# Attention values of 18 late pairs of tiles computed from rounded halves by three products instead of one full-precision product

## The chip, the cores and the metric

The kernel runs as one program on one core of a Trainium2 chip. The metric is device time in microseconds (us) of one execution, the median of several runs. A profiled execution has, beside its own time, a span: from the first to the last instruction that the trace shows. The engines are TensorE (PE, with its weight loads as PEld), VectorE (DVE), ScalarE (ACT), GpSimd (POOL) and SyncE (SP, which here only starts DMA transfers). Each works through its own list of instructions in order; semaphores make one wait for another.

## The reference

Attention over channels, then a mixture of experts with a greedy assignment by the sorted gate values:

```python
qn = q / (norm(q, axis=1) + 1e-6)            # q, k, v: (4, 5056, 256), float32
kn = k / (norm(k, axis=1) + 1e-6)
a = softmax(kn.transpose(0, 2, 1) @ qn / tau)   # 256 x 256 per batch
x = (v @ a).reshape(20224, 256)              # the attention values
logits = x @ w_gate                          # 8 experts
for idx in argsort(-logits.flatten()):       # greedy, at most 2528 tokens per expert
    tok, e = idx // 8, idx % 8
    if assigned[tok] < 0 and counts[e] < cap: assigned[tok] = e; counts[e] += 1
for e in range(8):
    out[assigned == e] = relu(x[assigned == e] @ w1[e]) @ w2[e]
```

The assignment depends on tiny differences of the gate values, so they are computed in full precision. The values x and the expert layers only have to be close to float32.

## The kernel before, in words

**Scores and gates.** For each of the four batches the kernel streams q and k, forms the 256 x 256 score matrix, the softmax and a matrix a that also holds the 8 gate columns (`a_f[b]`). Batch and chunk number name a piece of the tokens: (b, c) with 5 chunks of 1024 tokens per batch (8 tiles of 128). `L` collects the gate values of all tokens.

**Values.** v @ a is done per pair of tiles (`x_tiles`, lines 207 to 221): two tiles, each with two matmuls of 128 x 128 weights (v) and 256 moving columns (a) in float32, into one PSUM tile `px` (four of these rotate). The trace shows each float32 matmul as two PE instructions. ACT copies the pair to the chunk tile `xs` (two rotate), and after four pairs a DMA started by ACT stores the chunk into `x_d` in DRAM (`store_x`). The last 13 chunks, 52 pairs, are the list `TODO`; they run on PE while the routing of the first expert runs on DVE.

**Routing.** `route(p, R)` picks the tokens of one expert by two 16-ary searches for a threshold, four steps each. A step is: DVE compares all keys with 15 thresholds (`ge`, line 556), PE counts by 20 small matmuls (line 525), DVE reduces (`Dm`, `Dr`, `Ex`), PE sums by one matmul (line 538), DVE finds the new threshold (`mxs`, `hit`, `thr`, `cur`, `pre`). A ninth count follows. Then `ei`, the number of the expert, is known (its weights are loaded, `load_w`, on POOL's queue), and `compact` makes the list of its tokens: PE products `pi` (line 734), counted by ACT and DVE, then `src` (list to gather by) and `idx` (list to scatter by). Then the route of the next expert starts, beside the current expert's layers.

**Experts.** Each expert has 20 columns of 128 tokens, in chunks (the first expert: 2, 4, 4, 4, 4, 2 columns; the others five times 4). A column is gathered from `x_d` by an indirect DMA of POOL (`xg`, line 1032; 128 rows of 1 KB). A chunk is turned to channel-major by PE transposes (`turn`, line 1176, into the one PSUM tile `pt`) or by DVE and two DMAs, and split into a high half (ACT, rounded to fp32r) and a low half (DVE, the rest). A layer is three fp32r products, high by high, high by low, low by high: `layer1` (line 1219, 512 moving columns) and `layer2` (line 1253, 24 matmuls of 128 x 256 per column). ACT copies a column's result to `y`, and POOL scatters it with an indirect DMA (line 1262). Expert weights are split in the same way (`split_piece`: 4 pieces of 512 columns for each of w1 and w2; ACT line 1008, DVE line 1011).

**What sets the order.** All instructions are written out by one Python program that keeps a model of PE's and DVE's clocks (`Order`). `tick` moves the model's PE clock, and `hook` slips in whatever a stream (the route, the compaction) has ready by the model: DVE work by priority, PE work when its input is due. So each engine's list is fixed at build time, and where the model is wrong the chip waits. POOL's list is part of it: after each scatter of layer 2 one gather is taken from a queue (`gather`), and in layer 1 one for every second block of 128 hidden channels; with a list done, `load_ahead` puts the next chunk's columns into that queue. `next_turn` puts the transposes of the next expert's first chunk into the last chunk of layer 2 once the list is done and 7.5 us of the model's time have passed (`GATHER_LAT`).

## Time and profile before

| | |
|---|---|
| median of 3 runs | 1283.24 us (1282.59 to 1284.38) |
| the profiled execution's own time | 1284.13 us |
| its span | 1282.4 us |
| granted TensorE clock, mean | 0.996 |
| start to the last 13 chunks (scores, first chunks) | 0 to 231.7 us |
| last 13 chunks and the start of the first expert | 231.7 to 345.2 us |
| expert layers | 345.2 us to the end |

A row of the timeline gives start (us), length (us), engine, line, operation, output<-inputs, shapes and count, and in brackets how long the engine had been idle and what it waited for. A row of the windows gives a stretch, its length, and the busy time (and the number of instructions) of PE, PEld, DVE, ACT and POOL, then the granted clock, the DMA share and GB/s. A row of the waits reads: who waited for whom, us in total, times, longest.

### The profile page before, as it was taken

The numbers are of one execution on the slowest core, as the hardware profiler recorded it, in microseconds if no ns is written. First come the engines' busy times: TensorE is split into PE (matmuls) and PEld (weight loads), VectorE is DVE, ScalarE is ACT, GpSimd is POOL, SyncE is SP. The second block draws the span as 40 slices with busy tenths as digits, with TensorE's granted clock in tenths as the row PEclk, the third lists the DMA queues.
The fourth block names the chain that finished last, engine by engine and source line by source line (L and its number), as shares of the span: only waits on it lengthen the run. The fifth ranks groups of instructions, "written<-read, shape, count | busy, mean of one in ns | idle before, by whom it ended". The sixth has DMA issues, their size and how long they took to land.

```text
span 1282.4 us, 23001 instructions
## 1 busy us (share of the span) xinstructions
PE 1263.7 (99%) x8878; PEld 1124.4 (88%) x8878; DVE 806.3 (63%) x1992; ACT 530.0 (41%) x1197; POOL 388.9 (30%) x616
## 2 busy tenths in 40 slices
PE   7999999999999999999999999999999999999998
PEld 6888877787789998898999898988998998899998
DVE  6766396758677766967776787687665434344421
ACT  5554452225233443534443444354345434343331
POOL 1000010000152363265227333623543443433122
PEclk9999999999999999999999999999999999999999
DMA  8999885235324123333313341442352334323110
GB/s 297 359 402 351 298 280 194 73 129 197 124 86 144 38 78 107 116 102 111 132 60 118 101 161 39 151 159 67 104 167 78 114 101 148 109 71 109 64 52 33
DMA packets 80414, 180.38 MB, mean 141 GB/s; under 512 B 10800, under 2 KB 50608, under 8 KB 75696
## 3 DMA queue, kind: packets, MB, share of 16 engines
q1 hardware_dynamic: 41248, 99.63, 22.5%
q0 software_dynamic: 17664, 58.22, 13.9%
q10 hardware_dynamic: 21392, 21.06, 4.8%
q8 instruction: 69, 1.13, 0.4%
q14 instruction: 41, 0.34, 0.1%
HBM read 118.58 MB, written 60.29 MB: 139 GB/s over the span
## 4 chain that ended last, share of the span: by engine, by line
PE 85%; issue 8%; POOL 3%; DMA 3%; ACT 1%; DVE 1%; SPq 0%; POOLq 0%; ACTq 0%
PE ph L1219 30%; PE py L1253 29%; PE s L266 10%; PE px L216 10%; PE pc L525 3%; POOL out_dram L1262 2%; DMA ua<-in_q_dram 1%; PE px L371 1%; DMA x_d<-xs 1%; PE pi L734 0%; POOL xg L1032 0%; PE pt L734 0%; PE pm L356 0%; PE pc L284 0%; PE pc L538 0%
## 5 line engine op out<-in xcount | busy, mean ns | idle before, releaser
L1253 PE MATMUL py<-ua,hH 128*128 128x256 f32 (+1 forms) x2560 | 453.4, 280 | 0.0
L1219 PE MATMUL ph<-xH,ua 128*128 128x512 f32 (+3 forms) x1312 | 407.2, 386 | 0.1
L1253 PEld LDWEIGHTS py<-ua,hH 128*128 128x128 f32 (+1 forms) x2560 | 389.7, 187 | 2.3
L1253 PE MATMUL py<-ua,hL 128*128 128x256 f32 (+1 forms) x1280 | 356.5, 279 | 0.0
L1227 DVE SCALAR_TENSOR_TENSOR hL<-ph,hH 128x512 fp32r<-128x512 f32 (+3 forms) x328 | 219.3, 669 | 190.0 <-ACT hH L1222 186.6
L1262 POOL DMA_INDIRECT out_dram<-y,idx x160 | 161.7, 1011 | 445.4 <-ACT y L1260 388.8
L1222 ACT ACTIVATE hH<-ph 128x512 fp32r<-128x512 f32 (+3 forms) x328 | 190.9, 582 | 226.5 <-PE ph L1219 218.7
L1219 PEld LDWEIGHTS ph<-xH,ua 128*128 128x128 f32 x1312 | 242.9, 188 | 45.2 <-ACT xH L1178 0.6
L1219 PE MATMUL ph<-xL,ua 128*128 128x512 f32 (+3 forms) x656 | 253.1, 386 | 0.3 <-DVE xL L1181 0.2
L1253 PEld LDWEIGHTS py<-ua,hL 128*128 128x128 f32 (+1 forms) x1280 | 239.0, 187 | 0.0
L1260 ACT ACTIVATE y<-py 128x256 f32<-128x256 f32 (+1 forms) x160 | 61.4, 384 | 317.9 <-PE py L1253 274.3
L1032 POOL DMA_INDIRECT xg<-x_d,src x160 | 164.9, 1030 | 88.3 <-DVE Ex L534 42.9
L266 PE MATMUL s<-ua 128*128 128x256 f32 (+1 forms) x640 | 147.3, 390 | 7.4 <-DMA ua<-in_q_dram 7.2
L266 PEld LDWEIGHTS s<-ua 128*128 128x128 f32 (+1 forms) x640 | 123.6, 195 | 29.1 <-issue 12.0
L1219 PEld LDWEIGHTS ph<-xL,ua 128*128 128x128 f32 x656 | 123.3, 188 | 22.2 <-DVE xL L1181 0.8
L216 PE MATMUL px<-a,vr 128*128 128x256 f32 (+1 forms) x448 | 104.8, 389 | 0.1
L275 ACT ACTIVATE sq<-ua 128x1024 f32<-128x1024 f32 (+1 forms) x80 | 76.4, 969 | 58.8 <-DMA ua<-in_k_dram 22.4
L216 PEld LDWEIGHTS px<-a,vr 128*128 128x128 f32 x448 | 84.1, 193 | 12.0
L220 ACT ACTIVATE xs<-px 128x512 f32<-128x512 f32 (+1 forms) x96 | 50.0, 527 | 93.5 <-PE px L216 90.6
L1109 DVE TENSOR_TENSOR xL<-xT,xH 128x512 fp32r<-128x512 f32 (+1 forms) x72 | 47.5, 678 | 30.5 <-ACT xH L1106 30.3
L276 DVE TENSOR_TENSOR acc_k<-acc_k,sq 128x1024 f32<-128x1024 f32 (+2 forms) x40 | 44.4, 1114 | 27.1 <-ACT sq L275 25.9
L293 POOL TENSOR_SCALAR ny<-ny 128x4 f32<-128x4 f32 x4 | 1.3, 324 | 193.2 <-ACT ny L292 193.2
(284 smaller groups left out, 1136.8 us busy)
## 6 DMA issues: line engine op xcount, KB each, us to landing
x_d<-xs ACTq DMA_DIRECT2D x19, 1024.0 KB, 5.0
ua<-in_k_dram SPq DMA_DIRECT2D x35, 512.0 KB, 7.2
ua<-in_q_dram SPq DMA_DIRECT2D x35, 512.0 KB, 9.0
via<-xs SPq DMA_DIRECT2D x35, 512.0 KB, 2.9
xT<-via SPq DMA_DIRECT2D x140, 128.0 KB, 3.2
vr<-in_vt_dram SPq DMA_DIRECT2D x14, 1024.0 KB, 10.4
ua<-in_vt_dram SPq DMA_DIRECT2D x4, 1024.0 KB, 4.7
xg<-x_d,src POOLq DMA_INDIRECT x160
```

The lines of the kernel that those rows point to most:

```text
L216: mm = PE.matmul(px[:, i * C:i * C + width], lhsT=vs[b, c][:, kb, t + i, :], rhs=a_f[b][:, kb, 0:width], start=(kb == 0), stop=(kb == 1))
L220: S.activation(xs[:, t:t + n, 0:width], px[:, 0:n * width].rearrange("p (t c) -> p t c", t=n), AF.Copy)
L266: newest[0] = PE.matmul(sb[:, ib * C:(ib + 1) * C], lhsT=kt[:np_, t, ib * 128:(ib + 1) * 128], rhs=qt[:np_, t, :], start=(first and t == 0 ...
L275: S.activation(sq[:n, t0:t1], t_[:n, t0:t1], AF.Square)
L1032: P.indirect_dma_start(out=xg[:n, i, :], out_offset=None, in_=x_d, in_offset=bass.IndirectOffsetOnAxis(ap=idx[:n, col:col + 1], axis=0))
L1109: V.tensor_tensor(xL[:, kb, 0:k * 128].rearrange("p (i t e) -> p i t e", i=k, t=4), rows, xH[:, kb, 0:k * 128].rearrange("p (i t e) -> p i ...
L1219: PE.matmul(ph[:, 0:nt], lhsT=l[:, w], rhs=x_[:, kb, 0:nt], start=(i == 0), stop=(i == 5))
L1222: S.activation(hH[:, fb, 0:nt], ph[:, 0:nt], AF.Relu)
L1227: V.scalar_tensor_tensor(hL[:, fb, 0:nt], ph[:, 0:nt], 0.0, hH[:, fb, 0:nt].bitcast(F32), op0=OP.max, op1=OP.subtract)
L1253: PE.matmul(py[:n, 0:C], lhsT=l[:, fb, tk], rhs=w[:, d], start=(j == 0), stop=(j == 23))
L1260: S.activation(y[:n], py[:n, 0:C], AF.Copy)
L1262: sd = P.indirect_dma_start(out=out, out_offset=bass.IndirectOffsetOnAxis(ap=idx[:n, col:col + 1], axis=0), in_=y[:n], in_offset=None)
```

## The change

For chunks of batches 1 and 2 in `TODO`, once nine pairs have passed, a pair can be computed from halves (`x_halves`): v and a are each rounded to fp32r by ACT (`hi`, line 254 of the new kernel), the rest is formed by DVE (`lo`, line 256), and a pair is 12 fp32r matmuls (line 269) instead of 4 float32 ones. A stream (`halver`) makes the halves: its DVE step is of a new kind "L", which competes with the other streams as if it started 350 ns later (`YIELD`), at the lowest priority. Four pairs' halves fit in a ring on two of the tiles named `ua`; the halves of a (`a_hi`, `a_lo`) are in a new pool. A pair whose halves are not written by the time PE reaches it is computed as before. It comes to 18 such pairs; the list holds 20 high and 20 low halves of v and two of each for a, so two pairs of halves are made and not used. `TODO` starts with (3, 3) and (3, 4) now, whose tiles the ring takes over, and of the first expert's weights only the four pieces of w1 are split within the values; the four of w2 follow after the last pair.

```diff
@@ constants
-TODO = ((3, 1), (3, 2), (3, 3), (3, 4), (1, 2), (1, 3), (1, 4), (2, 0), (2, 1), (2, 2), (2, 3), (2, 4), (3, 0))
+TODO = ((3, 3), (3, 4), (3, 1), (3, 2), (1, 2), (1, 3), (1, 4), (2, 0), (2, 1), (2, 2), (2, 3), (2, 4), (3, 0))
+HALVED = (1, 2)
+RING = 4
+YIELD = 350
@@ after x_tiles
+    parts_a = {}
+    hv = []
+    ring = []
+    halved = {}
+    gone = []
+    live = []
+
+    def halver(work):
+        n = 0
+        for w in work:
+            while w not in gone and (len(gone) < 9 or len(live) >= RING):
+                yield "W", 0
+            if w in gone:
+                continue
+            b, c, t = w
+            if not ring:
+                for i in (2, 3):
+                    ring.append(ffw.tile([128, 2048], F32, name=f"ua{i}").bitcast(F32R)
+                                .rearrange("p (s h a t n) -> p s h a t n", s=2, h=2, a=2, t=2))
+            todo = []
+            if b not in parts_a:
+                parts_a[b] = [hv[0].tile([128, 2, C], F32R, name=x, bufs=2) for x in ("a_hi", "a_lo")]
+                todo.append((a_f[b][:, :, 0:C], parts_a[b]))
+            slot = ring[n // 2 % 2][:, n % 2]
+            n += 1
+            live.append(w)
+            todo.append((vs[b, c][:, :, t:t + 2, :], (slot[:, 0], slot[:, 1])))
+            for x, (hi, lo) in todo:
+                S.activation(hi, x, AF.Copy)
+                yield "L", 700
+                V.tensor_tensor(lo, x, hi.bitcast(F32), op=OP.subtract)
+            if w in gone:
+                live.remove(w)
+            halved[w] = todo[-1][1]
+
+    def x_halves(b, c, t, xs, tick):
+        px = ps_x.tile([128, 512], F32, name="px")
+        aH, aL = parts_a[b]
+        vH, vL = halved[b, c, t]
+        for i in range(2):
+            j = 0
+            for kb in range(2):
+                for l, r in ((vH, aH), (vH, aL), (vL, aH)):
+                    PE.matmul(px[:, i * C:(i + 1) * C], lhsT=l[:, kb, i, :], rhs=r[:, kb, :], start=(j == 0), stop=(j == 5))
+                    j += 1
+                    tick(C / 2.4 + 10)
+        S.activation(xs[:, t:t + 2, 0:C], px.rearrange("p (t c) -> p t c", t=2), AF.Copy)
@@ Order.hook
-                        c = (max(self.dve, st.mine) if eng == "V" else self.dve, st.prio(), st)
+                        c = ((max(self.dve, st.mine) if eng == "V" else self.dve) + (YIELD if eng == "L" else 0), st.prio(), st)
...
-                        self.dve = best[0] + st.next[1]
+                        self.dve = best[0] + st.next[1] - (YIELD if st.next[0] == "L" else 0)
@@ the last 13 chunks
+        hv.append(actx.enter_context(tc.tile_pool(name="hv", bufs=1, side="right")))
+        o.add(halver([(b, c, t) for b, c in TODO if b in HALVED for t in range(0, T, 2)]), lambda: 9)
         for i, (b, c) in enumerate(TODO):
             xs = vp.tile([128, T, GW], F32, name="xs", bufs=2)
             for t in range(0, T, 2):
-                x_tiles(b, c, t, xs, C, o.tick)
+                gone.append((b, c, t))
+                if (b, c, t) in halved:
+                    x_halves(b, c, t, xs, o.tick)
+                    live.remove((b, c, t))
+                else:
+                    x_tiles(b, c, t, xs, C, o.tick)
                 settle()
-                if cut_w[0] and o.pe > cut_w[0][0] and len(cut_w[0]) > 1:
+                if cut_w[0] and o.pe > cut_w[0][0] and len(cut_w[0]) > 1 and cut_w[0][1][0] == 0:
                     split_piece(0, *cut_w[0].pop(1))
```

Since all lists are written anew, other places move too. Three of them matter below.

VectorE, one step of the first search. Before:

```order
L556 TENSOR_TENSOR ge_1567<-hi_1598,thr_1686 128x10x120 x2
L567 TENSOR_SCALAR pre_1697<-steps_136,cur_1688 128x15
L528 TENSOR_TENSOR Dm_1725<-pc_1703,dmask_132 128x64
L531 TENSOR_REDUCE Dr_1728<-Dm_1725 128x8
L534 TENSOR_TENSOR Ex_1630<-Dr_1728,jsel_129 120x128
L545 TENSOR_REDUCE mxs_1736<-pc_1703 128x15
```

Now (ua2 and ua3 are the ring with the halves of v, vr a chunk of v):

```order
L607 TENSOR_TENSOR ge_1567<-hi_1601,thr_1696 128x10x120 x2
L618 TENSOR_SCALAR pre_1707<-steps_136,cur_1698 128x15
L256 TENSOR_TENSOR ua2_1677<-vr_726,ua2_1677 128x512 x2
L579 TENSOR_TENSOR Dm_1739<-pc_1713,dmask_132 128x64
L582 TENSOR_REDUCE Dr_1742<-Dm_1739 128x8
L585 TENSOR_TENSOR Ex_1633<-Dr_1742,jsel_129 120x128
L256 TENSOR_TENSOR ua3_1678<-vr_726,ua3_1678 128x512
L596 TENSOR_REDUCE mxs_1750<-pc_1713 128x15
```

Low halves stand in the two gaps of a step, ahead of `Dm`, which waits for the count on PE, and ahead of `mxs`, which waits for the sum.

GpSimd, from the last columns of the first expert's layer 2 on, where the second expert's list is done (scatters of `y` at line 1262, then 1313; gathers of `xg` at 1032, then 1083). Before, from the 13th scatter on (`xg_4071` is the second expert's first chunk, `xg_4072` its second; the copies to `spacer` tie a gather to a block of layer 1):

```order
L1262 DMA out_0_dram<-y_4067,idx_2504 20224x256
L1032 DMA xg_4071<-x_d_66,src_4000 128x256
L1261 MEMSET spacer_1566 1x1
L1262 DMA out_0_dram<-y_4113,idx_2504 20224x256
L1032 DMA xg_4071<-x_d_66,src_4000 128x256
L1043 COPY spacer_1566<-hH_4118 1x1
L1032 DMA xg_4071<-x_d_66,src_4000 128x256
L1043 COPY spacer_1566<-hH_4118 1x1
L1032 DMA xg_4071<-x_d_66,src_4000 128x256
L1043 COPY spacer_1566<-hH_4118 1x1
L1032 DMA xg_4072<-x_d_66,src_4000 128x256
```

Now, from the 17th scatter on (`xg_4400` is the second expert's first chunk, `xg_4401` its second; its first two gathers stand behind the 15th and 16th scatter):

```order
L1313 DMA out_0_dram<-y_4483,idx_2686 20224x256
L1083 DMA xg_4400<-x_d_66,src_4373 128x256
L1312 MEMSET spacer_1566 1x1
L1313 DMA out_0_dram<-y_4538,idx_2686 20224x256
L1083 DMA xg_4400<-x_d_66,src_4373 128x256
L1312 MEMSET spacer_1566 1x1
L1313 DMA out_0_dram<-y_4585,idx_2686 20224x256
L1083 DMA xg_4401<-x_d_66,src_4373 128x256
L1312 MEMSET spacer_1566 1x1
L1313 DMA out_0_dram<-y_4649,idx_2686 20224x256
L1083 DMA xg_4401<-x_d_66,src_4373 128x256 x3
L1083 DMA xg_4402<-x_d_66,src_4373 128x256 x4
```

The list comes two scatters later, and from there one gather goes with each scatter: the first chunk's fourth gather stands behind the 18th scatter, the second chunk's last three behind the 20th.

TensorE, around the 19th and 20th column of the first expert's layer 2 (`py_4543` and `py_4598`), where the first half of the second expert's first chunk is turned (`pt_4592`). Now:

```order
L1304 MATMUL py_4543<-ua2_2818,hH_4244 128x256
L1304 MATMUL py_4543<-ua3_2819,hH_4244 128x256
L1304 MATMUL py_4543<-ua2_2818,hL_4245 128x256
L1227 MATMUL pt_4592<-identr_72,xg_4400 128x128 x4
L1304 MATMUL py_4598<-ua2_2818,hH_4244 96x256
L1304 MATMUL py_4598<-ua3_2819,hH_4244 96x256
```

The four transposes, one for each gathered column, stand ahead of the 20th column as before; the second half is turned behind it, and the first half of the second chunk (`xg_4401`) after two blocks of layer 1, both as before. Further on, the third expert's second chunk is turned by eight PE transposes now (two times four, in layer 1), where DVE and DMAs turned it before; the list of PE has 44 transposes of `xg` instead of 36.

## The prediction

> **What bounds the kernel now.** I read the page first: busy time, and the chain of work that ended last.

> ```profile
> PE 1263.7 (99%) x8878; PEld 1124.4 (88%) x8878; DVE 806.3 (63%) x1992; ACT 530.0 (41%) x1197; POOL 388.9 (30%) x616
> PE 85%; issue 8%; POOL 3%; DMA 3%; ACT 1%; DVE 1%; SPq 0%; POOLq 0%; ACTq 0%
> ```

> TensorE is busy 99% of the span and carries the chain. So time goes down only where PE's list gets shorter, and every wait of PE that is added goes into the total. Then the windows, for the stretch of the first search and for the expert layers (length, then PE, PEld, DVE, ACT, POOL busy), and the longest of PE's waits between 231.7 and 345.2 us:

> ```profile
> 245.60:292.00 46.40, 46.40 (x374) 40.85 (x372) 28.38 (x108) 13.73 (x23) 0.00 (x0) 1.00 0.40 136
> 345.20:1282.40 937.20, 930.60 (x7052) 847.70 (x7051) 573.03 (x1456) 379.51 (x954) 370.64 (x580) 1.00 0.31 100
> ```

> ```profile
> PE pi L734 <- ACT ext L755: 2.1, 1, 2.1
> ```

> In the search PE is never idle, while DVE has 18.0 us free and ACT 32.7. Behind it PE is idle 6.6 us in 937, so nothing there absorbs a new wait.

> **The pairs.** First the copies of two pairs that no search step interrupts (ACT), then three matmuls of layer 2, whose shape (fp32r, 128 x 128 weights, 256 moving columns) is that of the new products:

> ```profile
> 233.74 0.60 ACT L220 ACTIVATE xs<-px 128x512 f32<-128x512 f32 x1 [6.89 <-PE px L216]
> 235.46 0.60 ACT L220 ACTIVATE xs<-px 128x512 f32<-128x512 f32 x1 [1.13 <-PE px L216]
> ```

> ```profile
> 386.23 0.39 PE L1253 MATMUL py<-ua,hH 128*128 128x256 f32 x2
> 386.45 0.28 PE L1253 MATMUL py<-ua,hL 128*128 128x256 f32 x1
> 386.57 0.39 PE L1253 MATMUL py<-ua,hH 128*128 128x256 f32 x2
> ```

> A pair takes 1.72 us now. Three products take 386.57 - 386.23 = 0.34, twelve 1.36. The gain is 0.36 a pair, **6.5 us** for 18.

> **The halves in the search.** A step of DVE, with PE's rows for the same step, and a high and a low half of the same size (weights, 128 x 512):

> ```profile
> 248.74 1.48 DVE L556 TENSOR_TENSOR ge<-hi,thr 128x1200 bf16<-128x1200 int16 x2
> 250.13 0.23 DVE L567 TENSOR_SCALAR pre<-steps,cur 128x15 f32<-128x15 f32 x1
> 251.55 0.23 DVE L528 TENSOR_TENSOR Dm<-pc,dmask 128x64 f32<-128x64 f32 x1 [1.19 <-PE pc L525]
> ...
> 252.99 0.28 DVE L545 TENSOR_REDUCE mxs<-pc 128x15 f32<-128x120 f32 x1 [0.58 <-PE pc L538]
> ```

> ```profile
> 250.76 0.75 PE L525 MATMUL pc<-oh,ge 128*128 128x64 bf16 x20
> ...
> 255.86 0.75 PE L525 MATMUL pc<-oh,ge 128*128 128x64 bf16 x20
> ```

> ```profile
> 318.30 0.62 ACT L1008 ACTIVATE ua<-ub 128x512 fp32r<-128x512 f32 x1
> 318.95 0.69 DVE L1011 TENSOR_TENSOR ua<-ub,ua 128x512 fp32r<-128x512 f32 x1
> ```

> A step is 5.1 us, and DVE idles 1.19 + 0.58 = 1.77 of it. Within the nine counts stand 20 low halves, 13.8 us by the row against 15.9 of gaps. Two ahead of `Dm` need 1.38 where 1.19 is free, one ahead of `mxs` 0.69 where 0.58 is: 0.3 over in a full step. The cover is that PE starts the count at 250.76, 0.54 behind the end of `ge` (250.22). What can break it is a low half that waits for its high half: ACT's list holds that behind a copy of a pair. A whole copy late (0.60) makes such a step 0.3 + 0.6 - 0.54 = 0.36 longer, eight steps 2.9; with no low half late the price is 0. PE's list has the counts at about the old spacing (10 float32 matmuls, or 37 to 38 products). Behind a waiting count stand the next pairs, so the wait is paid in full. I take **0.8**, nearer to the covered case, since DVE's total fits, and 0.2 for the second expert's first count, which stands five matmuls (5 x 0.43 = 2.2 us) nearer to the list's products than before, while three low weight halves (2.1) left DVE ahead of it. Together **1.0**, between 0 and 3. ACT's 22 high halves, 22 x 0.62 = 13.6, fit into its free time.

> **Stores and the end of the values.** Page, part 6, and the rows from the last store to the first chunk's transposes (ACT's queue, POOL, PE):

> ```profile
> x_d<-xs ACTq DMA_DIRECT2D x19, 1024.0 KB, 5.0
> ```

> ```profile
> 336.38 0.37 ACTq L226 DMA_DIRECT2D x_d<-xs  x1
> ```

> ```profile
> 339.73 0.95 POOL L1032 DMA_INDIRECT xg<-x_d,src  x1 [42.92 <-DVE Ex L534]
> 340.99 0.95 POOL L1032 DMA_INDIRECT xg<-x_d,src  x1 [0.30 <-issue]
> ```

> ```profile
> 343.79 0.28 PE L1176 MATMUL pt<-identr,xg 128*128 128x128 f32 x1 [0.76 <-DMA xg<-x_d,src]
> ```

> A chunk of four halved pairs takes 5.4 us without any step's PE work, and the copy that needs its `xs` tile back comes a pair later, at 6.8; a store lands in 5.0, so nothing waits. The 2.1 us wait for `ext` hangs on a store beside the weights' loads, which keep their place behind the search; I leave it. From the last store to the transposes the chain is store, gather, landing, all unchanged, so a gain of PE ahead of it comes through. The four pieces of w2 are split in that time now: one high half and four low ones, 0.62 + 4 x 0.69 = 3.4 us from 336.75, end at 340.1 on engines that are next needed after 343.79. They cost nothing; without that cover it would be 2.8. They issue no transfer. The new list for gathering stays far ahead:

> ```profile
> 323.33 0.18 DVE L832 COPY_PREDICATED src<-early,w__2476 128x20 int32<-128x20 int32 x1
> ```

> It is done 16.4 us before the first gather, and the gain takes at most 6.5 of that.

> **The second expert's gathers.** This is the place where I expect the gain to go. The lists show that its first chunk's fourth gather stands behind the 18th scatter now, and its second chunk's last three behind the 20th. The trace of before has both slots with other gathers in them. ACT's copy of the 18th column and POOL:

> ```profile
> 463.10 0.38 ACT L1260 ACTIVATE y<-py 128x256 f32<-128x256 f32 x1 [3.15 <-PE py L1253]
> ```

> ```profile
> 463.76 0.97 POOL L1262 DMA_INDIRECT out_dram<-y,idx  x1 [0.74 <-ACT y L1260]
> 465.04 0.97 POOL L1032 DMA_INDIRECT xg<-x_d,src  x1 [0.30 <-issue]
> ...
> 470.32 0.93 POOL L1262 DMA_INDIRECT out_dram<-y,idx  x1 [1.40 <-ACT y L1260]
> 471.56 0.98 POOL L1032 DMA_INDIRECT xg<-x_d,src  x1 [0.30 <-issue]
> ```

> And PE's transposes of the two chunks:

> ```profile
> 465.68 0.46 PE L1176 MATMUL pt<-identr,xg 128*128 128x128 f32 x4
> 465.97 0.45 PE L1253 MATMUL py<-ua,hH 128*96 128x256 f32 x2
> ...
> 469.47 0.50 PE L1176 MATMUL pt<-identr,xg 128*128 128x128 f32 x4
> ...
> 473.33 0.46 PE L1176 MATMUL pt<-identr,xg 128*128 128x128 f32 x4
> ```

> A gather that starts at 340.99 releases PE at 343.79: 2.80 us. The gather at 465.04 would release its transpose at 467.84, and PE is there at 465.68 + 0.2 for the other three: **1.9 us** of waiting. The next ones start at 471.56, and 1.26 apart (339.73, 340.99), the third at 474.08; it releases PE at 476.88, and PE is there at 473.33 + 0.2: **3.3 us**. The first wait moves the second place's scatter as well, so both are paid. Were the data there as POOL's 0.95 ends, the waits would be 0.1 and 1.5; a scatter can take 0.6 longer, then 2.5 and 3.9. I take 5.2, from the one row that has a landing, between 1.6 and 6.4.

> [...]

> **More transposes.** Eight more, two groups of 465.97 - 465.68 = 0.29: **0.6**.

> **Sum.** -6.5 + 1.0 + 5.2 + 0.6 = **+0.3 us**. The profiled execution took 1284.13 us, 1.73 more than its span and 0.89 more than the median; the change adds to either, so on the median 1283.24 it gives **1283.5**.

> **Rivals.**
> (a) The gathers are hidden anyway: the full gain stays, less the search and the transposes. For it: the model lets 7.5 us pass between the list and the turning. Against it: what is late is the queue of one gather per scatter, not the list. -6.5 + 1.0 + 0.6 = -4.9: 1278.3; with the waits at their low end, 1279.9.
> (b) Slower: the search becomes the bound. In each step the low halves at both gaps wait a whole copy: 0.3 + 1.2 - 0.54 = 0.96, eight steps 7.7 in place of 0.8, so +7.2: 1290.4. It decides from 0.39 a step on (3.1 in eight, then the total is over +2.6). For it: high halves are put on ACT just ahead of their low halves. Against it: ACT is busy 30% of that stretch, and a copy waits only for its pair.
> (c) The products do not run at 0.113. The page's weight loads of this shape last 0.187:

> ```profile
> L1253 PEld LDWEIGHTS py<-ua,hH 128*128 128x128 f32 (+1 forms) x2560 | 389.7, 187 | 2.3
> ```

> At that pace a pair takes 2.24, 0.52 more than now, and the total +16.2: 1299.4. The layer's rows, with the same loads, go against it.

> **How the numbers follow.** Forecast 0.60, its own range 1281.3 to 1286.7 (the search at 0 with the gathers' waits 1.2 shorter, at 3 with them 1.2 longer); (a) 0.22; (b) 0.15; (c) 0.03. A measurement of this kernel tells about 0.2%, 2.6 us, from no change. Faster: (a), and 0.04 of the forecast's low end, 0.26. Slower: (b), (c), and 0.03, 0.21. No change 0.53. The range takes in (a) and the upper bounds of the waits: 1278.0 to 1286.8.

> **What would show it.** Right: the last pair's copy some 5.5 us earlier; PE in the search idle under 3 us; a PE wait for the gather's DMA near 2 us ahead of the 20th column and one over 3 us in the second expert's first layer. Wrong: no such waits (a), waits of PE for `ge` or `Ex` in every step (b), or products 0.187 apart (c). A wait of PE elsewhere in the expert layers, or a longer one for `ext`, would be something that I have not seen.

## The result and the profile after

The changed kernel takes 1290.62 us (median of 6 executions), the kernel before 1284.34 beside it: a ratio of 1.0055, 95% interval 1.0041 to 1.0068. It is slower by 6 to 7 us. The prediction was 1283.5, with a range up to 1286.8, so it was wrong, and outside its range.

The profiled execution took 1290.05 us, its span is 1288.2. The page of the changed kernel, PE's busy time and the granted clock in 40 slices:

```profile
PE 1262.1 (98%) x8958; PEld 1125.0 (87%) x8958; DVE 816.0 (63%) x2012; ACT 544.0 (42%) x1219; POOL 388.1 (30%) x608
...
PEclk9999999999899999999999999999999999999999
```

PE's busy time fell by only 1.6 us (1263.7 before), while the span grew by 5.8. So PE waits more, and one slice shows a lowered clock. PE's waits over the whole span (us in total, times, longest):

```profile
PE pt L1227 <- DMA xg<-x_d,src: 7.4, 6, 2.2
PE pt L1227 <- DVE xL L1232: 2.2, 2, 1.3
PE pi L785 <- ACT ext L806: 1.9, 1, 1.9
```

The first row was 0.8 us before. To see where time went, I cut both spans at the same events of PE's list: the end of the gates, the last store of attention values, the first matmul of layer 1, the first of layer 2, the second expert's start (the last layer 2 block ahead of it), and its first layer-2 block. Windows of the kernel before, then of the changed one (stretch, length, PE, PEld, DVE, ACT and POOL busy, granted clock, DMA share, GB/s):

```profile
231.20:336.40 105.20, 102.22 (x697) 88.31 (x692) 78.56 (x238) 39.55 (x86) 4.38 (x3) 1.00 0.43 148
336.40:345.20 8.80, 7.11 (x49) 5.50 (x50) 4.10 (x13) 0.38 (x1) 4.25 (x5) 1.00 0.25 76
345.20:354.60 9.40, 8.00 (x80) 7.41 (x79) 5.21 (x13) 3.97 (x10) 2.80 (x5) 1.00 0.16 44
354.60:451.10 96.50, 96.50 (x777) 86.80 (x776) 73.51 (x201) 39.55 (x109) 38.81 (x61) 1.00 0.28 92
451.10:494.00 42.90, 42.67 (x322) 37.81 (x321) 30.61 (x72) 17.81 (x34) 24.20 (x36) 1.00 0.30 89
494.00:1081.80 587.80, 587.80 (x4536) 534.63 (x4535) 396.04 (x1069) 251.90 (x672) 246.19 (x380) 1.00 0.35 113
```

```profile
229.50:331.00 101.50, 99.18 (x768) 88.37 (x763) 86.29 (x247) 49.55 (x104) 4.36 (x3) 0.98 0.45 153
331.00:341.00 10.00, 6.74 (x30) 5.09 (x30) 5.78 (x15) 2.58 (x5) 4.71 (x5) 0.95 0.25 73
341.00:352.50 11.50, 10.22 (x80) 9.81 (x79) 5.20 (x13) 3.97 (x10) 2.57 (x5) 0.75 0.09 30
352.50:449.90 97.40, 96.84 (x777) 87.41 (x777) 72.46 (x193) 39.75 (x109) 34.03 (x55) 1.00 0.27 87
449.90:498.60 48.70, 43.39 (x323) 38.08 (x322) 31.42 (x80) 17.97 (x34) 27.78 (x38) 1.00 0.29 87
498.60:1088.10 589.50, 588.62 (x4565) 533.99 (x4564) 397.04 (x1079) 252.81 (x672) 246.50 (x375) 1.00 0.34 111
```

Line against line, after less before: -3.7 up to the last store, +1.2 from the store to the first layer, +2.1 in the first block of layer 1, +0.9 up to the second expert, **+5.8** around its start, +1.7 behind it. Up to the gates the changed kernel was 1.7 us ahead by chance (of the two profiles, only that of before has a stretch of half clock near 85 us), and the last 200 us gave 0.5 back; the sum is +5.8.

Two things stand out. The first is the +5.8. POOL's and PE's rows of the changed kernel around it:

```profile
463.75 1.53 POOL L1083 DMA_INDIRECT xg<-x_d,src  x1 [0.30 <-issue]
```

```profile
464.51 0.37 PE L1227 MATMUL pt<-identr,xg 128*128 128x128 f32 x3
467.12 0.28 PE L1227 MATMUL pt<-identr,xg 128*128 128x128 f32 x1 [2.23 <-DMA xg<-x_d,src]
...
474.53 0.22 PE L1227 MATMUL pt<-identr,xg 128*128 128x128 f32 x1
475.70 0.28 PE L1227 MATMUL pt<-identr,xg 128*128 128x128 f32 x1 [0.96 <-DMA xg<-x_d,src]
477.07 0.28 PE L1227 MATMUL pt<-identr,xg 128*128 128x128 f32 x1 [1.09 <-DMA xg<-x_d,src]
478.15 0.28 PE L1227 MATMUL pt<-identr,xg 128*128 128x128 f32 x1 [0.81 <-DMA xg<-x_d,src]
```

These are the two places that the prediction named: three transposes are done, the fourth waits 2.23 us for the gather behind the 18th scatter, and the second chunk waits 0.96 + 1.09 + 0.81 = 2.9 us. No half clock follows either.

The second is the clock. Two stretches of the changed kernel, with the clock in the third number from the right:

```profile
309.30:312.70 3.40, 3.40 (x10) 2.69 (x9) 3.40 (x8) 1.87 (x6) 0.00 (x0) 0.50 0.03 10
340.00:346.80 6.80, 6.10 (x42) 5.84 (x43) 2.19 (x6) 1.37 (x5) 2.02 (x3) 0.50 0.21 64
```

The first lies right behind PE's 1.9 us wait for `ext`, the second begins in the waits for the first chunk's gathers, and the first layer then runs slower: three of its products take 0.64 us there (342.93 to 343.57) and 0.36 behind it (347.14 to 347.50), and its first block 11.50 us, for what took 9.40. The kernel before waited as long for `ext` and kept its clock there; the last section returns to this.

### The profile page after: what moved, and what is told of

Read it like the earlier page. It is cut to its first block, busy times and chain, and to the rows that moved or that the text cites. A ratio compares the mean times of both kernels' runs of the same rounds, so it can differ in the third digit from the quotient of the medians.

```text
span 1288.2 us, 23198 instructions
## 1 busy us (share of the span) xinstructions
PE 1262.1 (98%) x8958; PEld 1125.0 (87%) x8958; DVE 816.0 (63%) x2012; ACT 544.0 (42%) x1219; POOL 388.1 (30%) x608
## 4 chain that ended last, share of the span: by engine, by line
PE 81%; issue 8%; DMA 4%; POOL 3%; DVE 2%; ACT 1%; SPq 0%; POOLq 0%; ACTq 0%; DVEq 0%
PE ph L1270 30%; PE py L1304 27%; PE s L317 9%; PE px L219 8%; PE pc L576 2%; POOL out_dram L1313 2%; DMA ua<-in_q_dram 2%; PE px L269 1%; PE px L422 1%; DMA x_d<-xs 1%; POOL xg L1083 1%; DMA xg<-x_d,src 1%; PE pi L785 0%; DVE ua L1062 0%; PE pt L785 0%
## 5 line engine op out<-in xcount | busy, mean ns | idle before, releaser
L1313 POOL DMA_INDIRECT out_dram<-y,idx x160 | 158.8, 993 | 424.6 <-ACT y L1311 383.5
L219 PE MATMUL px<-a,vr 128*128 128x256 f32 (+1 forms) x304 | 71.4, 391 | 0.1
L223 ACT ACTIVATE xs<-px 128x512 f32<-128x512 f32 (+1 forms) x78 | 39.3, 511 | 65.8 <-PE px L219 63.8
L219 PEld LDWEIGHTS px<-a,vr 128*128 128x128 f32 x304 | 57.8, 194 | 8.7
## 6 DMA issues: line engine op xcount, KB each, us to landing
x_d<-xs ACTq DMA_DIRECT2D x19, 1024.0 KB, 4.7
vr<-in_vt_dram SPq DMA_DIRECT2D x14, 1024.0 KB, 8.9
ua<-in_vt_dram SPq DMA_DIRECT2D x4, 1024.0 KB, 5.0
```

The lines of the kernel that those rows point to most:

```text
L219: mm = PE.matmul(px[:, i * C:i * C + width], lhsT=vs[b, c][:, kb, t + i, :], rhs=a_f[b][:, kb, 0:width], start=(kb == 0), stop=(kb == 1))
L1313: sd = P.indirect_dma_start(out=out, out_offset=bass.IndirectOffsetOnAxis(ap=idx[:n, col:col + 1], axis=0), in_=y[:n], in_offset=None)
```

## The experiments

Four of the runs were on a slower chip (1300.35 us for the kernel before), so each time is compared with the kernel before beside it only. Beside the median stand two numbers. The **clock loss** is the span times (1 - mean granted clock), averaged over the executions: the time that the lowered clock took, as an upper bound. In the changed kernel's profile it is one: of the 6.80 us of half clock from 340.00 PE was idle for 0.70, and three products took 1.8 times as long in them (0.64 in place of 0.36), not twice. The **rest** is the span less that loss.

| kernel | us | before beside it | ratio (95%) | rest, loss | rest, loss of before |
|---|---|---|---|---|---|
| changed, again | 1290.77 | 1284.27 | 1.0052 (1.0038-1.0065) | 1281.4, 7.7 | 1278.0, 4.5 |
| before, gathers late (second time) | 1291.38 | 1284.11 | 1.0057 (1.0043-1.0070) | 1284.2, 5.7 | 1277.8, 4.7 |
| before, gathers late (first time) | 1304.28 | 1300.35 | 1.0031 (1.0012-1.0050) | 1295.2, 7.4 | 1292.4, 6.0 |
| changed, gathers all at once | 1304.66 | 1300.35 | 1.0045 (1.0025-1.0065) | 1290.5, 12.5 | 1292.4, 6.0 |
| before, gathers all at once | 1310.42 | 1300.35 | 1.0093 (1.0061-1.0125) | 1293.8, 14.4 | 1292.4, 6.0 |
| new order, no halves | 1302.34 | 1300.35 | 1.0015 (0.9996-1.0035) | 1292.5, 7.7 | 1292.4, 6.0 |
| halves made, unused | 1291.27 | 1284.27 | 1.0052 (1.0039-1.0065) | 1284.1, 5.2 | 1278.0, 4.5 |
| changed, two gathers at a time | 1282.95 | 1284.27 | 0.9983 (0.9973-0.9994) | 1276.7, 3.7 | 1278.0, 4.5 |
| changed, waits filled | 1289.19 | 1284.27 | 1.0034 (1.0023-1.0045) | 1281.4, 5.2 | 1278.0, 4.5 |
| changed, two gathers and filled | 1282.60 | 1284.11 | 0.9986 (0.9976-0.9996) | 1277.6, 2.9 | 1277.8, 4.7 |
| the same, both chunks two at a time | 1282.04 | 1284.11 | 0.9980 (0.9971-0.9989) | 1276.8, 3.1 | 1277.8, 4.7 |
| before, waits filled | 1285.41 | 1284.11 | 1.0007 (0.9997-1.0016) | 1280.2, 3.3 | 1277.8, 4.7 |

**Theory**: the second expert's gathers come four to six places later, PE waits for them, and waits of PE bring half clock. **Rivals**: the halves on ACT and VectorE cost it; the new order of the pairs does; or the waits only show a delay that lies elsewhere.

### The late gathers, without any halves

The kernel before, with its gathers moved to the changed kernel's places; PE's, ACT's and DVE's orders stay:

```diff
         idx = routed[p]["src"]
...
+        if (p, c) == (1, 0):
+            queue.extend([lambda: None] * 6)
         for i, col in enumerate(cols_of(p, c)):
```

> The kernel before, with one edit: six empty places in the queue of gathers ahead of the second expert's, so that its first chunk's four gathers go behind the 15th to 18th scatter and its second chunk's behind the 19th and the 20th, as in the changed kernel. No halves, no products, no other order of pairs. Theory (late gathers): 5 to 6 us of waits for the gathers' DMA appear in the second expert's transposes, time 1289 to 1292 (1284.3 + 5.8, and up to 1.7 us for a stretch of half clock that such a wait may bring). Rival (the halves and their products are what costs): no more than 1 us slower than the kernel before.

> The kernel before with its second expert's gathers in the changed kernel's places (six empty places in the queue), once more beside the others of this call. Theory: 5 to 6 us of waits for the gathers' DMA in the second expert, and half clock behind some of them: 1289 to 1292, 0.4 to 0.6% above the kernel before. Rival (late gathers cost only their waits' time less what they hide): 1286 or less.

On the slower chip it is 0.31% slower (interval 0.12 to 0.50), less than the 0.4 to 0.6% expected; on the other 0.57%, as much as the changed kernel (0.52 to 0.55%). PE's waits from 345 us on, and the window of the second expert's start, in the second of these runs:

```profile
PE pt L1178 <- DMA xg<-x_d,src: 4.6, 4, 1.8
```

```profile
453.00:501.30 48.30, 43.47 (x322) 38.00 (x321) 30.70 (x72) 18.05 (x34) 28.04 (x40) 1.00 0.28 88
```

The stretch takes 48.3 us, against 42.9 before and 48.7 in the changed kernel. Late gathers alone make the kernel before as slow as the change does, and only POOL's list differs. In the profile of the first run half clock of 3.4 us followed at 471.3 and at 484.9, right behind these waits; in that of the second none followed them.

### Earlier gathers: all at once

The changed kernel, and the kernel before, with this in `load_x`:

```diff
         xgs[p, c] = xg
+        if (p, c) in ((1, 0), (1, 1)):
+            while queue:
+                gather()
```

> The changed kernel, but the gathers of the second expert's first two chunks are issued one behind the other as soon as its list is there (all nine in the queue behind the 15th scatter) instead of one per output column; PE's, ACT's and DVE's orders are unchanged. Theory (late gathers): in the changed kernel's profile PE's transposes of these two chunks take 7.05 us from first to next against 1.22 before, so 5.8 us go here, and the time falls from 1290.6 to 1284 to 1286, about the kernel before; the four waits for the gathers' DMA (5.1 us) are gone. Rival (the gathers only show a delay that lies elsewhere, in the search or in the halves): the waits go but another wait of the same size comes in the second expert, and the time stays within 2 us of 1290.6. Rival (the granted clock is the loss): the waits go, and the time falls by more than 5.8 us, to 1282 or less, because stretches of half clock go with them.

> The kernel before, with the gathers of the second expert's first two chunks issued at once when its list is there. Theory: in the kernel before these gathers land ahead of the transposes (no wait for them is in its profile), so no change, 1283 to 1285.5. Rival (gathers that stand one behind the other on POOL hold back the scatters and so the output tiles): slower than 1286.

The waits for the second expert's gathers went, but the changed kernel so edited is 0.45% above the kernel before, about as far as without the edit on other chips (0.52 to 0.55%), and the kernel before even lost 0.9% (there the lists of PE, ACT and DVE changed too). New waits came in their place. The changed kernel so edited, window 445 to 475 us:

```profile
DVE Dm L579 <- remote: 15.1, 1, 15.1
ACT y L1314 <- remote: 14.0, 1, 14.0
...
PE pc L589 <- DVE Ex L585: 10.1, 1, 10.1
```

And the kernel before so edited, window 440 to 470:

```profile
ACT hH L1225 <- remote: 12.8, 2, 8.2
...
PE ph L1222 <- issue: 10.1, 2, 6.8
```

ACT and DVE stand still at the same time, for something that no instruction of the kernel releases ("remote"), and PE behind them. That the row of gathers is the cause is not shown. Waits named "remote" stand in all four profiles of this slower chip, without such a row too (up to 3.7 us with late gathers, up to 4.8 us in the new order without halves), and in none of the ten profiles from other chips; with the row the longest are 15.1 and 8.2 us, and these begin while it runs. Late packets of instructions do not explain them either, as far as the traces have them. The page has two queues of the kind `instruction`; in the changed kernel (packets, MB, share of 16 engines):

```profile
q8 instruction: 70, 1.15, 0.4%
q14 instruction: 40, 0.33, 0.1%
```

That is 16 KB a packet on q8 and 8 KB on q14. In the first of these runs ACT and DVE go on at 470.5 and 470.2 us, before the next packet of the two queues starts (473.2), and the changed kernel has 25.1 us without the start of such a packet (463.1 to 488.2) and no standstill. The expectations (1284 to 1286, and no change for the kernel before) failed, and these runs could not tell whether the old waits were the loss.

### Earlier gathers: two at a time

```diff
-        for i, col in enumerate(cols_of(p, c)):
-            queue.append(lambda i=i, col=col, n=n_in(col): fetch(i, col, n))
+        step = 2 if (p, c) == (1, 0) else 1
+        cs = list(enumerate(cols_of(p, c)))
+        for g in range(0, len(cs), step):
+            queue.append(lambda g=g: [fetch(i, col, n_in(col)) for i, col in cs[g:g + step]])
```

> The changed kernel itself, run again so that the next three stand beside it on the same chip. Expected: 0.3 to 0.8% slower than the kernel before (0.55% in its first measurement), with waits of 4 to 7 us for the gathers' DMA in the second expert's transposes, and a lower mean granted clock than the kernel before.

> The changed kernel, but the second expert's first chunk is gathered by two gathers behind each of the 15th and 16th scatter instead of one behind each of the 15th to 18th; its second chunk then goes behind the 17th to 20th. PE's order is unchanged. Theory (late gathers): the waits for these gathers (5.8 us in the profile) fall to under 1 us and the time to 5 to 6 us below the changed kernel beside it, within 0.2% of the kernel before. Rival (what held DVE, ACT and PE up when nine gathers were issued in a row comes with two in a row as well): the waits go, but a stretch of 3 us or more in which DVE and ACT stand still comes between 450 and 475 us, and less than half of the 5.8 us is gained.

The changed kernel came out as before (1290.77). Two gathers behind each of the 15th and 16th scatter bring 1282.95: 7.8 us less than the changed kernel beside it, and 0.17% less than the kernel before (interval 0.06 to 0.27). PE's wait for gathers from 345 us on:

```profile
PE pt L1229 <- DMA xg<-x_d,src: 1.1, 1, 1.1
```

By the means of the table the rest fell by 4.7 us, as the waits did (5.1 to 1.1, where under 1 was expected, and their small gaps), and the clock loss by 4.0. No standstill came. The expected 5 to 6 us were too few, since they held next to nothing for the clock. Which waits the clock loss hung on is open: no half clock follows the second expert's waits in the two profiles of the changed kernel.

### The clock

15 more idle matmuls around the first chunk's transposes, where PE waits; they compute nothing that is used:

```diff
+        busy.append((idle, 5, 6, 4))
         turn(0, 0, 0)
         turn(0, 0, 1)
+        busy.clear()
...
             n = n_in(col)
+            if busy and (kb, i) != (1, 1):
+                for _ in range(busy[0][1 + 2 * kb + i]):
+                    PE.matmul(busy[0][0], lhsT=wt[0, 0][0][:, 0:128], rhs=wt[0, 0][0][:, 512:1024], start=True, stop=True)
             PE.transpose(
```

> The changed kernel with 15 more idle matmuls of 512 columns around the first chunk's four transposes, where PE waited 3.3 us in all (5 ahead of the first, 6 ahead of the second, 4 ahead of the third): PE stays busy while it waits, and nothing else changes. Theory (a share of the loss is the granted clock): the 6.8 us of half clock that followed these waits in the changed kernel's profile do not come, the first layer starts at full pace, and the time falls by about 2 us (9.4 us instead of 11.5 us from the first matmul of the first layer to the first of the second), with a mean clock that is 0.002 higher. Rival (the clock has its own course): half clock comes as often as without, and the time stays within 1 us.

> The kernel before with the same 15 idle matmuls around the first chunk's four transposes, where its PE waits 1.7 us in all. Theory (the clock falls after waits of PE, and the changed kernel has more of them there): little to gain, 0 to 1 us below the kernel before. Rival (filling gains the same everywhere, so the clock is no part of the difference between the two kernels): 1.5 to 2.5 us below the kernel before.

The changed kernel so filled takes 1289.19, 1.6 us less (the two intervals of the table overlap). Its rest is the same to 0.1 us (1281.4); its clock loss is 5.2 in place of 7.7. The windows of its store-to-layer stretch and of the first block of layer 1:

```profile
329.40:339.30 9.90, 9.90 (x44) 7.56 (x45) 5.77 (x15) 2.58 (x5) 4.60 (x5) 1.00 0.24 71
339.30:348.70 9.40, 7.99 (x79) 7.40 (x79) 5.21 (x13) 3.97 (x10) 2.67 (x5) 1.00 0.13 39
```

The first stretch is as long as without filling (9.9 against 10.0): PE waits as long, but busily. The block after it takes 9.40 in place of 11.50. So the 2.1 us there were the clock's, and idle time of PE is what brought it: none of the four profiles with filled waits has half clock between the last store and the end of this block, and eight of the ten without filling have. In the kernel before, filling did not pay: its clock loss fell by 1.4 us, but the rest grew by 2.4. Most of that is the filling itself, which ends after the gather has landed: the first transpose starts 2.01 us after POOL's second gather ends, 0.87 without filling, and the stretch from the last store to the first layer takes 10.4 us in place of 8.8. Neither expectation was met (0.07% slower, interval -0.03 to 0.16).

### Both, and both chunks

> The changed kernel with both edits that gained: the second expert's first chunk by two gathers behind the 15th and the 16th scatter, and 15 idle matmuls around the first chunk's transposes. Theory (late gathers and granted clock are two separate losses): the sum of both gains, 7.8 us and 1.6 us below the changed kernel, so 1281 to 1282.5 where the kernel before takes 1284.3, with a mean clock of 0.998. Rival (they are the same loss): 1283, as with the two gathers alone.

> As the kernel with two gathers at a time and filled waits, but the second expert's second chunk too is gathered two at a time, behind the 17th and 18th scatter: eight gathers and four scatters in a row of four columns. Theory (late gathers): the last wait for a gather in the second expert (1.4 us) goes, and the time falls by 1 to 1.5 us against the kernel with two gathers for the first chunk alone. [...]

Two gathers and filled waits together take 1282.60, between the two expectations. The gains do not add up: by the ratios there is none over two gathers alone (0.9986 against 0.9983, on different chips). Against the kernel before, the clock loss is lower by 1.8 in place of 0.8, but the rest by 0.2 in place of 1.3; why is not shown. The last kernel has `step = 2` for both chunks of the second expert. Its stretch of the second expert's start shows that the waits are gone, and no standstill comes:

```profile
449.40:492.20 42.80, 42.58 (x321) 37.90 (x321) 31.57 (x75) 18.50 (x35) 27.98 (x40) 1.00 0.33 101
```

42.8 us is what the kernel before takes (42.9). POOL's queue is as full there as in the run with all gathers at once (one transfer each 1.3 us from 451 to 473), but scatters stand between the gathers, two by two. Whether that or the chip makes the difference stays open. At 1282.04 us this is the lowest time of all: 0.20% under the kernel before (interval 0.11 to 0.29). Over two gathers for the first chunk alone, 1 to 1.5 us were expected; the ratios differ by 0.03% (0.9983, on another chip), and 1282.60 beside it by 0.6 us, less than these runs can tell.

### The order of the pairs, and the halves

No pair halved: `HALVED = ()`, the order of the pairs and the late pieces of w2 stay.

> The changed kernel with no pair halved: what stays is the new order of the pairs and that the pieces of w2 are split after the last pair. Its gathers stand behind the same scatters as in the kernel before. Theory: same time as before, 1283 to 1285.5, no wait over 1 us for a gather in the second expert. Rival (the order of the pairs or the moved pieces of w2 cost time): over 1286.

0.15% above the kernel before, with an interval that holds zero, and the same rest (1292.5 against 1292.4). The order of the pairs costs nothing that can be seen.

Halves made by ACT and VectorE, and all pairs computed from the unrounded tiles:

```diff
                 if (b, c, t) in halved:
-                    x_halves(b, c, t, xs, o.tick)
                     live.remove((b, c, t))
-                else:
-                    x_tiles(b, c, t, xs, C, o.tick)
+                x_tiles(b, c, t, xs, C, o.tick)
```

> The changed kernel, but all pairs are computed from the unrounded tiles: ACT and VectorE still make the same halves in the first search, and nobody reads them. Its gathers stand behind the 14th to 16th scatter, as in the kernel before. Theory (the halves hardly cost): the search is up to 2 us longer, the time 0 to 3 us above the kernel before. Rival (the halves on ACT and VectorE are what makes the change slow): 5 us or more above the kernel before, with waits between the search's steps.

1291.27, 7 us above the kernel before: a miss. PE's waits in its search:

```profile
PE pc L576 <- DVE ge L607: 1.9, 4, 0.9
```

With pairs of the old length, the five steps that hold halves take 6.64, 5.89, 5.51, 6.31 and 5.03 us in the trace, 29.4 in all, against 25.0 before; in the changed kernel the same five take 26.0. From the end of the gates to the last store this kernel needs 3.4 us more than the kernel before (108.6 against 105.2). So the halves are not free in these lists; in the changed kernel, whose lists differ, PE shows no wait of 0.15 us or more in the same steps. That they are not what makes it slow, two gathers at a time show: there the halves stay and the loss goes. The other half of this kernel's 7 us lies behind the last store, among it 1.4 us of wait for a gather of the first expert, and 6.8 us of half clock in the first layer; this I did not take apart.

## Why the prediction was wrong

**Pairs and search** (terms -6.5 and +1.0, together -5.5): right in sum, but by luck. The five profiles with halved pairs that had no half clock in this stretch (the four kernels with two gathers or filled waits, and all at once) need 99.0 to 99.4 us from the end of the gates to the last store, the six of the kernel before, its edits and the new order without halves 104.4 to 105.4: -5.6 between the means. Rows of the products:

```profile
262.39 0.40 PE L269 MATMUL px<-a_hi,ua 128*128 128x256 f32 x2
262.62 0.28 PE L269 MATMUL px<-a_lo,ua 128*128 128x256 f32 x1
262.75 0.40 PE L269 MATMUL px<-a_hi,ua 128*128 128x256 f32 x2
```

Three take 0.36, not 0.34, so a pair takes 1.43 and gains 0.30: 5.4 us for 18, not 6.5. The search's last five steps grew by 0.9, but PE, which has pairs to do meanwhile, shows no wait of 0.15 us or more there, so of the +1.0 next to nothing was paid; 0.2 of the -5.6 is a shorter wait for `ext`. Two misses of about 1 us, one each way, cancel. Rival (b) is out for the changed kernel, rival (c) as well.

**The second expert's gathers** (term +5.2): right in both places. Counted as in the prediction, from where PE could have started the last transpose, the first wait is 467.12 - (464.51 + 0.2) = 2.4 (1.9 predicted) and the second 478.15 - (474.53 + 0.2) = 3.4 (3.3); together 5.8, by which the stretch grew. The gather in the 18th's place took 3.37 us from its start (463.75) to the transpose (467.12), where I had 2.80 from one row; the second chunk's last took 2.79 (475.36 to 478.15). Rival (a), that the gathers are hidden anyway, is out: with late gathers alone the kernel before loses as much as by the whole change.

**The first step that failed is "from the last store to the transposes the chain is store, gather, landing, all unchanged, so a gain of PE ahead of it comes through".** Rows of the changed kernel, to be held against those at 336.38, 339.73 and 340.99 of before:

```profile
330.95 0.37 ACTq L277 DMA_DIRECT2D x_d<-xs  x1
```

```profile
335.07 1.05 POOL L1083 DMA_INDIRECT xg<-x_d,src  x1 [38.01 <-DVE hit L600]
336.43 1.21 POOL L1083 DMA_INDIRECT xg<-x_d,src  x1 [0.30 <-issue]
```

The store now takes 4.12 us until the first gather starts, 3.35 before, and the two gathers take 0.36 longer. This is the same in all seven profiles of the changed program and its edits that keep the halved pairs (4.13 to 4.20 in the others). What came late is the store's landing: of its sixteen landing signals fifteen come within 2.4 to 2.55 us of its start, as before, and the last after 3.27 to 3.34, where it came after 2.50 in the kernel before; in all fourteen profiles the gather starts 0.86 us behind the last signal. In each of the seven a packet of 16 KB of the queue q8 (`instruction`) starts 0.1 to 0.35 us behind the last store (331.22 here) and one of 8 KB of q14 1.6 to 2.1 us later; in the kernel before none starts from 328.5 to 344.4. With a packet of 8 KB alone beside the store (halves made, unused) the last signal comes after 2.64. So a packet of q8 beside the store goes with the late landing in every one of these profiles, but no edit tested whether it is the cause. It cost 1.2 us of waiting, and 2.1 more by the clock followed. Not all of this 2.1 belongs to the longer waits: with the old, shorter ones, 3.4 us of half clock came at this place in two of the four unfilled profiles of the kernel before and its edits (at 345.0 and 345.8, both with late gathers); with the longer ones it was 3.4 to 6.8 us, in all four.

**The second step that failed is a term at nothing: the sum had none for the clock**, and this is its largest gap. I read the clock as 1.00 in every stretch that I quoted and took it as given. Of the 6.5 us between the two kernels in the second measurement, up to 3.3 are clock loss (7.7 against 4.5) and 3.4 are rest. The rest, by the profiles, is -5.6 (pairs and search), +5.8 (second expert), +1.2 (the chain), +0.9 (between the first layer and the second expert), and +1.7 (behind it), less 0.5 at the end: +3.5. Of the +0.9, 0.6 is a wait of PE that the sum had nothing for, in the shifted lists:

```profile
423.23 0.50 PE L1270 MATMUL ph<-xH,ua 128*128 128x512 f32 x1 [0.56 <-DVE hL L1278]
```

**Eight more transposes** (+0.6): the stretch behind the second expert's start holds them, two groups of 0.3; three waits of PE that were not there before (for `ge`, `xH` and `xL`) add 0.8, and with shifted search steps it is +1.7 in all.

So of the 6.2 us between the forecast of +0.3 and these 6.5, some 3 are costs that the sum lacked or had too small (the chain 1.2, the two stretches beside the second expert's start 2.0, its gathers 0.6, less 0.5 at the end), and up to 3.3 are the clock's.

## What to carry to other kernels

In this kernel, where PE is busy for 98% of the span, PE's waits of 1 to 2 us had two prices: their own, and a chance of half clock behind them (between the last store and the end of layer 1's first block in eight of ten profiles without filled waits, in none of four with them). A change that saves PE time at one place and adds short waits at others should be charged for both, or the waits filled with matmuls: in the changed kernel that took 1.6 us off, with intervals that overlap; in the kernel before, where the filling made the first transpose start 2.01 us behind the gather's end in place of 0.87, it did not pay. The gain ahead of the paced queue of transfers (5.6 us) went into waits for that queue (5.8) as long as its gathers stood where they did: two at a time was enough here, 7.8 us less than the changed kernel; nine in a row, on a slower chip, came with a standstill of two engines (up to 15.1 us) whose cause is open. When work moves between engines' lists, look at which of the paced slots (here one gather per scatter) the last transfer of a chunk lands in, before anything else.

## What the runs showed of the hardware

```profile
303.70:307.10 3.40, 2.83 (x14) 2.24 (x13) 2.97 (x6) 0.57 (x5) 0.00 (x0) 1.00 1.06 374
307.10:310.50 3.40, 1.83 (x10) 1.65 (x10) 1.54 (x3) 3.40 (x12) 0.00 (x0) 1.00 0.40 141
```

```profile
305.90:309.30 3.40, 1.45 (x9) 1.07 (x8) 1.68 (x3) 1.56 (x5) 0.00 (x0) 1.00 0.88 310
```

No run set the position of a wait, and busy time is not the whole measure: the half clock at 160.28 in the kernel before follows a step in which PE was busy throughout (3.40), in part with matmuls of 1 and 8 columns. In the changed kernel's step at `ext` PE was idle for 1.95 of the 3.40 us.
- **Spread.** Mean clocks of single executions of the changed kernel lay between 0.992 and 0.995, those of the filled one between 0.994 and 1.000, and the fastest execution of the filled kernel (1283.82) is 7 us below its slowest, with the clock loss between 0 and 7.7 us: most of this kernel's spread is the clock's. It is not so for all: in the new order without halves, on the slower chip, the rest moved by 8.7 us and the loss by 5.2.
- **Waits of one chip.** On the chip where the kernel before takes 1300.35 us, in place of 1284, ACT and DVE have five or six waits of 1 to 15 us in each of the four profiles that no instruction of the kernel releases; in the ten profiles from other chips there is none.
- **One late signal of sixteen.** A store of 256 KB with a packet of 16 KB of q8 beside it landed 0.8 us later than without one (3.27 us behind its start, in place of 2.50), by the last of its sixteen signals alone.
